# A recurrence in chunks with mixture of depths: PSUM of the state as two tiles, W1 copied by one operation, and the state's chain ahead in the plan

## Chip, cores and metric

The kernel runs on one core of one Trainium2 chip. The metric is device microseconds of one execution of the whole program. Before the change the median of three runs is 329.27 us (327.18 to 331.36).

## What is computed

The first half is a delta rule over 768 tokens for 4 batches of 8 heads with 48 columns each; the second takes the 128 best tokens of each batch through a small expert.

```python
k_n = k / (norm(k) + 1e-6)
for t in range(S):                        # state: 48 x 48 for each batch and head
    y[t] = q[t] @ state
    v_old = state.T @ k_n[t]
    state = state + beta[t] * outer(k_n[t], v[t] - v_old)
x = y of all heads side by side           # (4, 768, 384)
scores = x @ w_gate
out = x
for b in range(4):                        # the 128 tokens of highest score
    xe = x[b, top]
    out[b, top] = xe + sigmoid(scores[b, top]) * (relu(xe @ w1) @ w2)
```

## The kernel before, in words

**Units.** The tokens go in chunks of 64. A unit `i` is one chunk of two batches with all heads (16 pairs of batch and head); there are 24, units 0 to 11 for batches 0 and 1, units 12 to 23 for batches 2 and 3. Within one such half the state goes from unit to unit, so the units of a half run one after the other. Four units make a group `e` (six groups).

**Preparation** (`prep`). q and k are loaded by DMA, turned by TensorE (L399) and copied by ScalarE (L412). TensorE makes the products of k with k (L448, L458), ScalarE copies them to `g` (L464), and from the second group on they go through DRAM (`gd`, L468, L533) to be laid out anew as `a`. The products of q with k (L458 again) are masked on VectorE (L471) to `p`.

**Elimination** (`eliminate`). VectorE inverts the triangular 32x32 blocks of a whole group, row by row (L577, L591, L597), and ends with L602 and in groups 0, 1 and 5 with a transpose (L605). From group 1 on the result comes back by DMA as `tt`, in groups 2 to 4 by way of DRAM (`ad`, L609, L615). `join` makes `z` from it (L679) and copies it to `zt` (L683). Units 0 to 4 and 20 are "direct": they read the result in `g`, by smaller matmuls (L761).

**The chain of the state** (`recur`). For each unit, in this order:
- `mm_r` (L733): the state times k, added in PSUM (`psta`) onto v, which VectorE has scaled and written there (L707); two halves `h4`, each in a bank of its own. The first unit of a half has none.
- `out_r` (L743): ScalarE copies each half to `v`.
- `mm_w` (L755, direct L761): the inverse times that, in two halves, to a PSUM tile `pair`.
- `out_w1` (L779, L781): ScalarE copies the part that the second step needs to `w1`: 96 partitions at once, and two pieces of 32 that change partition.
- `mm_m` (L773): `zt` times `w1` is added; `out_w` (L785) copies the sum to `wbd` in two halves.
- `mm_s` (L795): k times that is added onto the state in `psta`, and `out_s` (L802) copies the state to SBUF in four pieces. The last unit of a half has neither.
- Beside the chain, `mm_q` (L812) and `mm_p` (L824) make the unit's output, L830 copies it, VectorE forms the scores (L842), and L835 writes it out.

**Ranking and expert.** `ranking` compares the scores (L918 to L986) on all engines; `depths` finds the tokens' numbers (L1004), gathers the rows (L1027), turns them (L1033), multiplies by `w1_sb` (L1046) and `w2_sb` (L1062), and scatters the result (L1073). Batches 0 and 1 can start once units 0 to 11 are ranked.

**The order of the work** is made ahead, by a planner in the kernel. Every operation is given to it with its engine, an assumed duration, the operations that it depends on, and a priority (a lower number comes first). `order` plays the program through with these durations, and the instructions are put in each engine's queue in the order of the planned starts; every queue then runs in that order. `pick` takes among the operations that could start first the one of lowest priority; an operation that is marked `hard` keeps later-priority work from starting where that would hold it up by over 0.2 us. The chain is hard. Before, its priority is `u = 10 * i`; q's turn has `10 * i - 20`, the products of q `10 * i - 14`, z `10 * i - 30`, the preparation of group e `40 * e - 100` and its elimination `40 * e - 50`; `mm_q` and `mm_p` have `u + 3`, the ranking of batches 0 and 1 has 148 to 149.2, the expert of batches 0 and 1 260 and more. The planner fills planned gaps of TensorE with matmuls of ones whose result nobody reads (L304).

Of the kernel before, what the change touches and what calls it, by code (L numbers as in the profile page):

```python
# [15 lines left out]
P = 128  # L16
# [141 lines left out]
def kernel(  # L158
# [41 lines left out]
    def sbuf(name, shape, dt=FP32):  # L200
        return const.tile([P] + shape, dt, name=name)
# [41 lines left out]
    rings["one"] = [psum.tile([P, 512], FP32, name=f"one{m}") for m in range(2)]  # L243
    plan.ring("pair", 2)
    plan.ring("one", 2)
    psta = psum.tile([P, 2, 512], FP32, name="psta")

    def got(*key):
        name, m = plan.live[key]
# [38 lines left out]
    nnT = [sbuf(f"nnT{m}", [HC]) for m in range(3)]  # L288
    bh = [sbuf(f"bh{m}", [HC]) for m in range(2)]
    tmp = [sbuf(f"tmp{m}", [HC * HC // 4]) for m in range(2)]  # L290
    w1 = sbuf("w1", [GI, D])
    wbd = [sbuf(f"wbd{m}", [GP, 2, D]) for m in range(2)]
    sts = [sbuf(f"s{m}", [GP, 2, D]) for m in range(2)]
    junk = sbuf("junk", [DM], BF16)
# [21 lines left out]
    four = [(0, 0), (1, 1), (0, 1), (1, 0)]  # L316

    def zero():
        nc.vector.memset(psta[:, :, :GI * D], 0.0)

    def constants():
        nc.vector.memset(warm, 1.0)
# [12 lines left out]
        nc.gpsimd.iota(iota_r, pattern=[[1, CAP]], base=0, channel_multiplier=0,  # L335
                       allow_small_or_imprecise_dtypes=True)

        for b in range(2):
            nc.tensor.matmul(psta[:, b], lhsT=warm[:, :P], rhs=warm, start=True, stop=True)
        zero()  # L340
        nc.vector.memset(pair, 0.0)
        for t in wbd + sts:
# [74 lines left out]
    def prep(i):  # L417
# [89 lines left out]
        else:  # L507
# [3 lines left out]
            n["sg"] = sp(0.6, spill, n["eg"], u, take=[("gd", e)] * (i % BC == 0), lat=4.6)  # L511
            n["sg"].own = 4.2
        v = 10 * i - 14
        n["w"] = pe(0.52, products("qt", kw), n["eq"] + n["ek"] + [N.get(("end", 0))], v,
                    work=1024, take=[kw, ("p", i)], lat=LATE["p"])
        n["ep"] = [dve(0.62, out_p, [n["w"]], v - 200, give=[kw])]

# [174 lines left out]
    def values(i, after):  # L692
        g, c = divmod(i, NCH)
        e, ch = divmod(i, BC)
        n = N[i]

        def vh():
            t = got("v", i)
            by = nnT[e % 3][:, ch * GP:(ch + 1) * GP, None].to_broadcast([P, GP, D])
            if c == 0:  # L700
                nc.vector.tensor_tensor(out=t, in0=t, op=ALU.mult, in1=by)
                return
            to = psta[:, :, GI * D:2 * GI * D].rearrange("p h (b r d) -> p h b r d", b=2, d=D)
            for h in range(2):
                x, y = [z.rearrange("p (h r b) d -> p h b r d", h=2, b=2)[:, h]
                        for z in (t, by)]
                nc.vector.tensor_tensor(out=to[:, h], in0=x, in1=y, op=ALU.mult)  # L707

        n["lv"] = sp(1.38, load(i, "v", (nc.sync,) * 2), prio=10 * i - 35,
                     take=[("v", i)], lat=5.0 if i < 2 else LATE["v"])  # L710
        n["vh"] = dve(0.68 if c > 0 else 0.5, vh, [n["lv"], N["e", e]["nt"], *after],
                      10 * i - 60 if c == 0 else 10 * i - 400)

    def recur(i):
# [3 lines left out]
        hard = dict(hard=True)  # L718
        n, o = N[i], R.get(i - 1, {})
        r = R[i] = {}  # L720
        wb, s_old, s_new = wbd[i % 2], sts[(i + 1) % 2], sts[i % 2]
        kw, ky = ("pair", i, "W"), ("one", i, "Y")

# [4 lines left out]
        def mm_r(h4):  # L728
            def emit():
                for par in range(2):  # L730
                    for bb in range(2):
                        r = bb * 2 + h4
                        nc.tensor.matmul(  # L733
                            psta[half[bb], h4, (GI + 2 * par) * D:(GI + 2 * par + 2) * D],
                            lhsT=got("kt", i)[:, r, half[par]],
                            rhs=s_old[:, r * 2 + par].rearrange("p h d -> p (h d)"),
                            start=False, stop=True, skip_group_check=True)
            return emit


        def out_r(h4):
            def emit():
                nc.scalar.copy(got("v", i)[:, h4 * GI:(h4 + 1) * GI].rearrange("p x d -> p (x d)"),  # L743
                               psta[:, h4, GI * D:2 * GI * D])
            return emit

        def mm_w(h4):
            def emit():
                x, pw = got("v", i), heads(kw)
                for y in range(2 * h4, 2 * h4 + 2):  # L750
                    for bb, par in four:
                        a = 2 * y + par
                        xa = a if c == 0 else y // 2 * 4 + par * 2 + y % 2
                        if not n["direct"]:
                            nc.tensor.matmul(pw[half[par], bb, y],  # L755
                                             lhsT=got("tt", e)[half[bb], ch * GP + a],
                                             rhs=x[half[bb], xa], start=(y == 0), stop=False,
                                             skip_group_check=True)
                            continue
                        for rows in (lo, hi):  # L760
                            nc.tensor.matmul(pw[rows[par], bb, y],  # L761
                                             lhsT=got("g", e)[rows[bb], ch * GP + a, HC:],
                                             rhs=x[rows[bb], xa], start=(y == 0), stop=False,
                                             skip_group_check=True)
            return emit


        def mm_m():
            zt, pw = got("zt", i), heads(kw)
            for y in range(GI):  # L770
                for bb, par in four:
                    rows = at[bb][par]
                    nc.tensor.matmul(pw[hi[par], bb, y], lhsT=zt[rows, y], rhs=w1[rows, y],  # L773
                                     start=False, stop=True, skip_group_check=True)


        def out_w1():
            pw = heads(kw)
            nc.scalar.copy(w1[:3 * HC], pw[:3 * HC, 0])  # L779
            for par in range(2):  # L780
                nc.scalar.copy(w1[hi[par]], pw[lo[par], 1])  # L781

        def out_w(par):
            def emit():
                nc.scalar.copy(wb[half[par], :, par].rearrange("p (b r) d -> p b r d", b=2),  # L785
                               heads(kw)[half[par]])
            return emit

        def mm_s(h4):
            def emit():  # L790
                t = got("k", i)
                for bb in range(2):
                    for rt in range(2):
                        a = bb * 4 + h4 * 2 + rt
                        nc.tensor.matmul(psta[half[rt], h4, bb * 2 * D:(bb + 1) * 2 * D],  # L795
                                         lhsT=t[:, a], rhs=wb[:, a].rearrange("p h d -> p (h d)"),
                                         start=False, stop=True, skip_group_check=True)
            return emit

        def out_s(h4, rt):  # L800
            def emit():
                nc.scalar.copy(  # L802
                    s_new[half[rt], :, rt].rearrange("p (b h x) d -> p b h x d", b=2, h=2)[:, :, h4],
                    psta[half[rt], h4, :GI * D].rearrange("p (b x d) -> p b x d", b=2, d=D))
            return emit

        def mm_q():
# [42 lines left out]
        x = n["vh"]  # L850
        xs = [x]
        if c > 0:
            r["r"] = [pe(0.41, mm_r(h4), [*o["es"][h4], *o["w"], x], u, work=768, **hard)
                      for h4 in range(2)]
            r["xr"] = xs = [act(0.2, out_r(h4), [r["r"][h4]], u, **hard) for h4 in range(2)]
        if i + 1 < NU:
            values(i + 1, [*r.get("xr", []), *o.get("xr", [])])
        clear = N[i + 1]["vh"] if i + 1 < NU else None
# [13 lines left out]
        prev2 = R.get(i - 2, {})  # L872
        r["mw"] = []
        for h4 in range(2):
            r["mw"].append(pe(0.33 if n["direct"] else 0.28, mm_w(h4),
                              [xs[h4 % len(xs)], *n["bk"], *o.get("w", []), *r["mw"]], u,
                              give=[("v", i)] + [("tt", e)] * (e > 0) + [("g", e)] * n["direct"],
                              take=[kw] if h4 == 0 else [], work=384, **hard))
        e1 = act(0.6, out_w1, [*r["mw"], o.get("mm")], u, **hard)
        r["mm"] = pe(0.45, mm_m, [e1, *n["ez"]], u, give=[("zt", i)], work=192, **hard)  # L880
        r["w"] = [act(0.42, out_w(par), [r["mm"], prev2.get("p"), *prev2.get("s", [])], u,
                      give=[kw], **hard) for par in range(2)]
        if not late:
            r["s"] = [pe(0.41, mm_s(h4), [*r["w"], *sum(o.get("es", []), []),
                                          *sum(prev2.get("es", []), []), clear, N.get("zero")],
                         u, work=768, **hard) for h4 in range(2)]
            r["es"] = [[act(0.2, out_s(h4, rt), [r["s"][h4], o.get("q"), *o.get("r", [])], u, **hard)
                        for rt in range(2)] for h4 in range(2)]
        plan.add("PE", 0.0, lambda: None, [*r.get("s", []), n["tk"]], 10 * i, give=[("k", i)])
        qdep = [*r["w"], *r.get("s", [])]  # L890
        pdep = None
        if c > 0:
            r["q"] = pdep = pe(0.81, mm_q, [*sum(o["es"], []), *n["eq"], *r["w"]], u + 3,
                                 take=[ky], work=768)
        r["p"] = pe(0.81, mm_p, [*qdep, *n["ep"], pdep], u + 3, work=1536,
                    take=[] if c > 0 else [ky], give=[("kt", i), ("qt", i), ("p", i)],
                    lat=LATE["x"] if i < NU - 1 else 0.22)
        outs()
# [259 lines left out]
```

## Time and profile before

| | |
|---|---|
| median of 3 runs | 329.27 us (327.18 to 331.36) |
| the profiled execution, its own time | 326.44 us |
| its span, first to last instruction | 324.7 us |
| granted TensorE clock | 0.967 |
| TensorE matmuls busy | 280.9 us (87%) |
| VectorE busy | 220.0 us (68%) |
| ScalarE busy | 159.2 us (49%) |
| GpSimd busy | 26.8 us (8%) |

A line of groups names the source line, the engine and the operation, what is written and what is read (out<-in, buffer numbers left out), partitions x elements, the number of instructions; then their busy time, the mean of one in ns, and the engine's idle time before them with what ended it. A line of the timeline has the start (us from the span's start), the length, the engine, the line, the operation and the count, and in brackets the idle time before it and what ended that. A matmul in fp32 shows as two instructions, so L733 of one unit has 16. PE is TensorE, DVE is VectorE, ACT is ScalarE. In rows of 40 slices each digit is the busy share of a slice of 8.1 us in tenths. The first line that a prediction shows for an operation gives its line number, by which it is found in the code.

### The profile page before, as it was taken

What the parts mean: (1) busy time and instruction counts of PE and PEld (TensorE: products, weight loads), DVE (VectorE), ACT (ScalarE), POOL (GpSimd) and SP (SyncE); (2) the same over time, 40 slices, a digit from 0 to 9 for tenths busy, and PEclk for the clock granted to TensorE, in tenths of its full rate; (3) what the DMA queues carried; (4) which work ended last, traced back from release to release, by engine and by line L of the source; (5) the groups of instructions that cost most, each with busy time, mean ns of one, the idle gap of its engine ahead of it and who ended that gap; (6) DMA issues with size and microseconds to landing.
All of it is one profiled execution on the core that took longest, in us unless ns stands there. A gap on an engine that the chain in (4) does not pass through costs nothing. (4 is left out here: it accounts for less than half of the span.)

```text
span 324.7 us, 16721 instructions
## 1 busy us (share of the span) xinstructions
PE 280.9 (87%) x7306; PEld 205.8 (63%) x7362; DVE 220.0 (68%) x859; ACT 159.2 (49%) x435; POOL 26.8 (8%) x51
## 2 busy tenths in 40 slices
PE   7779997889979898789968898889988889999993
PEld 3545645676657666467647676677767777586571
DVE  6159999998988799969994788997535323432000
ACT  2235415667644765457535566556647647211110
POOL 8111002000100020001000100000020000031011
PEclk9879999999987999889999999999979999999999
DMA  6876978473788758926987993335332021120000
GB/s 99 157 131 153 233 155 142 82 181 58 199 175 143 197 153 177 178 42 151 226 180 139 257 178 64 76 71 96 82 76 52 2 52 25 28 66 36 2 26 24
DMA packets 127545, 37.04 MB, mean 114 GB/s; under 512 B 119536, under 2 KB 123760, under 8 KB 127472
## 3 DMA queue, kind: packets, MB, share of 16 engines
q1 hardware_dynamic: 119904, 33.13, 47.1%
q10 hardware_dynamic: 7056, 1.26, 2.3%
q0 software_dynamic: 512, 1.57, 1.5%
q8 instruction: 58, 0.95, 1.2%
q14 instruction: 15, 0.12, 0.1%
HBM read 22.58 MB, written 12.32 MB: 107 GB/s over the span
## 5 line engine op out<-in xcount | busy, mean ns | idle before, releaser
L304 PE MATMUL one<-warm 128*128 128x512 bf16 x195 | 58.7, 403 | 6.5 <-issue 5.9
L591 DVE TENSOR_TENSOR tmp<-a 128x29 f32<-128x29 f32 (+8 forms) x162 | 55.1, 340 | 0.0
L597 DVE TENSOR_TENSOR a<-a,tmp 128x29 f32<-128x29 f32 (+8 forms) x162 | 53.9, 333 | 0.0
L577 DVE SCALAR_TENSOR_TENSOR a<-a 128x28 f32<-128x28 f32 (+29 forms) x198 | 46.1, 241 | 0.1
L802 ACT COPY s<-psta 64x192 f32<-64x192 f32 x88 | 27.7, 314 | 22.7 <-PE psta L795 21.4
L304 PEld LDWEIGHTS <-warm 128*128 128x128 bf16 x252 | 20.6, 100 | 23.1 <-issue 6.8
L707 DVE TENSOR_TENSOR psta<-v,nnT 128x192 f32<-128x192 f32 x44 | 16.1, 366 | 19.6 <-ACT v L743 18.9
L785 ACT COPY wbd<-pair 64x384 f32<-64x384 f32 x48 | 22.8, 474 | 12.1 <-PE pair L773 9.5
L1046 PE MATMUL pair<-xeT,w_sb 128*64 128x128 f32 x384 | 23.5, 275 | 2.3 <-ACT hT L1053 2.2
L560 POOL TENSOR_SCALAR_AFFINE_SELECT mb<-bh 128x1024 f32<-128x1024 f32 x6 | 10.6, 1759 | 165.8 <-DVE a L602 90.2
L938 DVE TENSOR_SCALAR_CACHE_REDUCE mk<-rep 128x64 bf16<-128x64 f32 (+10 forms) x22 | 13.4, 610 | 15.0 <-ACT rep L931 15.0
L1046 PEld LDWEIGHTS pair<-xeT,w_sb 128*64 128x64 f32 x384 | 20.9, 137 | 3.8 <-ACT hT L1053 3.1
L1062 PE MATMUL one<-w_sb,hT 128*64 128x384 f32 x128 | 22.6, 491 | 0.0
L773 PE MATMUL pair<-w,zt 32*32 32x48 f32 x768 | 13.9, 208 | 9.5 <-ACT w L781 8.7
L795 PE MATMUL psta<-wbd,k 128*64 128x96 f32 x352 | 20.9, 262 | 1.1 <-issue 0.5
L743 ACT COPY v<-psta 128x192 f32<-128x192 f32 x44 | 13.3, 330 | 16.4 <-PE psta L733 16.3
L795 PEld LDWEIGHTS psta<-wbd,k 128*64 128x64 f32 x352 | 16.4, 144 | 7.0 <-ACT wbd L785 4.7
L464 ACT COPY g<-pair 128x512 f32<-128x512 f32 x24 | 13.9, 588 | 13.1 <-PE pair L448 8.2
L773 PEld LDWEIGHTS pair<-w,zt 32*32 32x32 f32 x768 | 10.4, 107 | 15.3 <-ACT w L781 13.9
L824 PE MATMUL one<-wbd,p 128*64 128x96 f32 x384 | 20.0, 247 | 0.0
L1068 DVE SCALAR_TENSOR_TENSOR xe<-one,gate,xe 128x384 f32<-128x384 f32 x4 | 2.5, 617 | 24.8 <-PE one L1062 24.7
L812 PE MATMUL one<-s,qt 128*64 128x96 f32 x352 | 18.6, 248 | 0.0
(116 smaller groups left out, 475.8 us busy)
## 6 DMA issues: line engine op xcount, KB each, us to landing
gd<-g SPq DMA_DIRECT2D x20, 256.0 KB
q<-in_q_dram SPq DMA_DIRECT2D x48, 96.0 KB
v<-in_v_dram SPq DMA_DIRECT2D x48, 96.0 KB
out_dram<-x SPq DMA_DIRECT2D x20, 192.0 KB
k<-in_k_dram SPq DMA_DIRECT2D x36, 96.0 KB
a<-gd SPq DMA_DIRECT2D x20, 128.0 KB
w_sb<-in_moe_w_dram SPq DMA_DIRECT2D x3, 512.0 KB
ad<-a SPq DMA_DIRECT2D x3, 512.0 KB
```

What stands on the lines that cost most here:

```text
L304: nc.tensor.matmul(to if name == "one" else to[:, 0], lhsT=warm[:, :P], rhs=warm, start=True, stop=True)
L577: nc.vector.scalar_tensor_tensor(out=to, in0=of, scalar=by, in1=to, op0=ALU.mult, op1=ALU.add)
L591: nc.vector.tensor_tensor(out=view(), op=ALU.mult, in0=x[0].to_broadcast(shape), in1=x[1].to_broadcast(shape))
L597: nc.vector.tensor_tensor(out=to, in0=to, in1=view(), op=ALU.add)
L773: nc.tensor.matmul(pw[hi[par], bb, y], lhsT=zt[rows, y], rhs=w1[rows, y], start=False, stop=True, skip_group_check=True)
L785: nc.scalar.copy(wb[half[par], :, par].rearrange("p (b r) d -> p b r d", b=2), heads(kw)[half[par]])
L795: nc.tensor.matmul(psta[half[rt], h4, bb * 2 * D:(bb + 1) * 2 * D], lhsT=t[:, a], rhs=wb[:, a].rearrange("p h d -> p (h d)"), start=False, ...
L802: nc.scalar.copy(s_new[half[rt], :, rt].rearrange("p (b h x) d -> p b h x d", b=2, h=2)[:, :, h4], psta[half[rt], h4, :GI * D].rearrange(" ...
L812: nc.tensor.matmul(got(*ky)[half[bb], :2 * GI * D] .rearrange("p (h r x d) -> p h x r d", h=2, r=2, x=2)[:, h4, par], lhsT=got("qt", i)[:, ...
L824: nc.tensor.matmul(py[half[bb], x * 2 * D:(x + 1) * 2 * D], lhsT=t[:, a], rhs=wb[:, a].rearrange("p h d -> p (h d)"), start=(c == 0 and x ...
L1046: nc.tensor.matmul(ps[half[x]], lhsT=w1_sb[:, t, c0:c0 + C], rhs=got("xeT", b)[:, t], start=(t == 0), stop=(t == KD - 1))
L1062: nc.tensor.matmul(got("one", b, "o")[c0:c1, :DM], lhsT=got("hT", b)[:, f, c0:c1], rhs=w2_sb[:, f], start=(f == 0), stop=(f == KF - 1))
```

## The change

There are three edits. The state's PSUM `psta`, one tile of two banks, becomes two tiles of one bank each, and every use of `psta[:, h4]` becomes `psta[h4]`. The second batch's part of W (bank 1) now begins at column 0 and the first's (bank 0) at column 192; in the units that are not direct, `mm_w` makes the part of the second batch that `w1` needs once more, on the partitions where it is wanted, in columns 192 to 383 of bank 1. So `out_w1` is one copy of 128 partitions and 2 x 192 columns there, and `w1` has a place for each of the two batches. Direct units keep three copies. Last, the chain's operations get the priority `uc = u - 35`, and most of its assumed durations are altered. `mm_q` and `mm_p` keep `u + 3`.

```diff
-    psta = psum.tile([P, 2, 512], FP32, name="psta")
+    psta = [psum.tile([P, 512], FP32, name=f"psta{h}") for h in range(2)]
...
-    w1 = sbuf("w1", [GI, D])
+    w1 = sbuf("w1", [2, GI, D])
+    bank0, bank1 = GI * D, 512
...
-        for b in range(2):
-            nc.tensor.matmul(psta[:, b], lhsT=warm[:, :P], rhs=warm, start=True, stop=True)
+        for t in [*psta, *[t[:, 1] for t in rings["pair"]]]:
+            nc.tensor.matmul(t, lhsT=warm[:, :P], rhs=warm, start=True, stop=True)
...
-        n["w"] = pe(0.52, products("qt", kw), n["eq"] + n["ek"] + [N.get(("end", 0))], v,
+        n["w"] = pe(0.58, products("qt", kw), n["eq"] + n["ek"] + [N.get(("end", 0))], v,
...
+        uc = u - 35
...
+        def w_of(bb):
+            x = got(*kw).rearrange("p b x -> p (b x)")[:, (bank1, bank0)[bb == 0]:]
+            return x[:, :GI * D].rearrange("p (r d) -> p r d", d=D)
...
+                    for par in range(0 if direct else 2):
+                        a = 2 * y + par
+                        xa = a if c == 0 else y // 2 * 4 + par * 2 + y % 2
+                        nc.tensor.matmul(again[hi[par], y], lhsT=t[half[1], ch * GP + a, :HC],
+                                         rhs=x[half[1], xa], start=False, stop=True,
+                                         skip_group_check=True)
...
         def out_w1():
-            pw = heads(kw)
-            nc.scalar.copy(w1[:3 * HC], pw[:3 * HC, 0])
+            if not n["direct"]:
+                nc.scalar.copy(w1.rearrange("p b r d -> p b (r d)"),
+                               got(*kw)[:, :, GI * D:2 * GI * D])
+                return
+            nc.scalar.copy(w1[:3 * HC, 0], w_of(0)[:3 * HC])
             for par in range(2):
-                nc.scalar.copy(w1[hi[par]], pw[lo[par], 1])
+                nc.scalar.copy(w1[hi[par], 1], w_of(1)[lo[par]])
...
-            r["r"] = [pe(0.41, mm_r(h4), [*o["es"][h4], *o["w"], x], u, work=768, **hard)
+            r["r"] = [pe(0.38, mm_r(h4), [*o["es"][h4], *o["w"], x], uc, work=768, **hard)
                       for h4 in range(2)]
-            r["xr"] = xs = [act(0.2, out_r(h4), [r["r"][h4]], u, **hard) for h4 in range(2)]
+            r["xr"] = xs = [act(0.22, out_r(h4), [r["r"][h4]], uc, **hard) for h4 in range(2)]
...
-            r["mw"].append(pe(0.33 if n["direct"] else 0.28, mm_w(h4),
-                              [xs[h4 % len(xs)], *n["bk"], *o.get("w", []), *r["mw"]], u,
+            r["mw"].append(pe(0.33 if n["direct"] else 0.37, mm_w(h4),
+                              [xs[h4 % len(xs)], *n["bk"], *o.get("w", []), *r["mw"]], uc,
...
-        e1 = act(0.6, out_w1, [*r["mw"], o.get("mm")], u, **hard)
-        r["mm"] = pe(0.45, mm_m, [e1, *n["ez"]], u, give=[("zt", i)], work=192, **hard)
-        r["w"] = [act(0.42, out_w(par), [r["mm"], prev2.get("p"), *prev2.get("s", [])], u,
+        e1 = act(1.0 if n["direct"] else 0.38, out_w1, [*r["mw"], o.get("mm")], uc, **hard)
+        r["mm"] = pe(0.47, mm_m, [e1, *n["ez"]], uc, give=[("zt", i)], work=192, **hard)
+        r["w"] = [act(0.47, out_w(par), [r["mm"], prev2.get("p"), *prev2.get("s", [])], uc,
...
-            r["s"] = [pe(0.41, mm_s(h4), [*r["w"], *sum(o.get("es", []), []),
+            r["s"] = [pe(0.36, mm_s(h4), [*r["w"], *sum(o.get("es", []), []),
...
-            r["es"] = [[act(0.2, out_s(h4, rt), [r["s"][h4], o.get("q"), *o.get("r", [])], u, **hard)
+            r["es"] = [[act(0.32, out_s(h4, rt), [r["s"][h4], o.get("q"), *o.get("r", [])], uc, **hard)
...
-            r["q"] = pdep = pe(0.81, mm_q, [*sum(o["es"], []), *n["eq"], *r["w"]], u + 3,
+            r["q"] = pdep = pe(0.68, mm_q, [*sum(o["es"], []), *n["eq"], *r["w"]], u + 3,
...
-        r["p"] = pe(0.81, mm_p, [*qdep, *n["ep"], pdep], u + 3, work=1536,
+        r["p"] = pe(0.76, mm_p, [*qdep, *n["ep"], pdep], u + 3, work=1536,
```

## The prediction, as put on record

> **What bounds the kernel now.** I read the page, then the timeline of TensorE (PE) and ScalarE (ACT) around one unit, then the start times of each unit's stages, then the waits for DMA, then the tail. The page:
>
> ```profile
> span 324.7 us, 16721 instructions
> ...
> PE   7779997889979898789968898889988889999993
> ...
> DVE  6159999998988799969994788997535323432000
> ...
> L304 PE MATMUL one<-warm 128*128 128x512 bf16 x195 | 58.7, 403 | 6.5 <-issue 5.9
> ```
>
> TensorE looks full, but 58.7 us of it are L304, matmuls that only fill planned gaps. VectorE is dense until slice 27 (222 us), where the sixth elimination ends. So in between I must see whether the units wait for VectorE or for each other. One unit (16) in the timeline; start, length, engine, line:
>
> ```profile
> 202.67 0.88 PE L795 MATMUL psta<-wbd,k 128*64 128x96 f32 x16
> 203.38 0.83 PE L812 MATMUL one<-s,qt 128*64 128x96 f32 x16
> 203.59 1.29 ACT L802 COPY s<-psta 64x192 f32<-64x192 f32 x4 [0.51 <-PE psta L795]
> 204.04 0.83 PE L824 MATMUL one<-wbd,p 128*64 128x96 f32 x16
> 204.80 0.46 PE L399 MATMUL pair<-ident,q 64*128 64x64 f32 x8
> 205.19 0.88 PE L733 MATMUL psta<-s,kt 128*64 128x96 f32 x16
> 206.12 0.32 ACT L743 COPY v<-psta 128x192 f32<-128x192 f32 x1 [1.23 <-PE psta L733]
> 206.71 0.60 ACT L412 COPY qt<-pair 128x512 f32<-128x512 f32 x1
> 207.18 0.35 ACT L743 COPY v<-psta 128x192 f32<-128x192 f32 x1
> 207.62 0.45 PE L755 MATMUL pair<-v,tt 64*64 64x48 f32 x16
> 208.21 0.32 ACT L779 COPY w<-pair 96x192 f32<-96x192 f32 x1 [0.68 <-ACT v L743]
> 208.56 0.64 ACT L781 COPY w<-pair 32x192 f32<-32x192 f32 x2
> 209.25 0.54 PE L773 MATMUL pair<-w,zt 32*32 32x48 f32 x32 [0.70 <-ACT w L781]
> 209.73 1.25 PE L304 MATMUL one<-warm 128*128 128x512 bf16 x5
> 210.91 0.45 PE L679 MATMUL pair<-tt,g 32*32 32x32 f32 x32
> 211.29 0.88 PE L795 MATMUL psta<-wbd,k 128*64 128x96 f32 x16
> ```
>
> The cycle takes 8.62 us (202.67 to 211.29). The first ACT copy of `psta` at 206.12 follows the end of all 16 matmuls of L733 (206.07), though it needs the first eight only, and the two copies L743 have L412 between them. L824 and L399 stand ahead of L733, L679 ahead of L795. Stage by stage (first L755/L761 of a unit): unit 12 at 172.8, 16 at 206.5, 20 at 245.4, 23 at 273.3, and its L830 ends at 279.5. Unit 20 needs only the sixth elimination, done by 221.9 (L605), and starts 23.5 us later: from unit 12 on the units wait for each other. Before that they wait for VectorE and DMAs (units 4, 5, 8). Unit 11 is different:
>
> ```profile
> 164.40 0.45 PE L679 MATMUL pair<-tt,g 32*32 32x32 f32 x30 [0.64 <-DMA tt<-ad]
> ...
> 166.02 0.68 PE L755 MATMUL pair<-v,tt 64*64 64x48 f32 x32
> ```
>
> Its copies L743 ended at 160.7, but L755 stood behind L679 of units 12 and 13, which waited for a DMA. Last, the tail: three batches of the expert run from 284.2 to 319.8 with little gap, 11.85 us each, and the span ends 5.0 us later. So TensorE's order sets the end.
>
> **The skill.** TensorEngine Tiling (Array Packing), Key Properties: changing the tiling mode drains TensorE. The trace agrees: 64x64 matmuls of L755 start in groups of four 58 ns apart, but from 64x128 (L399) to 64x64 (L458) 151 ns pass, from L755 to L399 149 ns. PSUM — Partial Sum Buffer, PSUM bank collisions raise a hardware error: engines collide on one bank and quadrant, different banks run clean. So the wait of L743 for the second half of L733 comes from the tile's being one, not from the chip. ScalarE: Activation LUTs, What ACT_TABLE_LOAD costs: 186 ns + 0.833 ns per element, 506 ns for 384; the trace has 487 ns for 128x384 (L830), which I use.
>
> **The change, part by part**, for one cycle.
> 1. *Two tiles.* L743 may follow the first eight matmuls of L733, L802 those of L795. First saving 0.41 us (half of L733's 0.83 to the end). The second is counted in 2. If the split does nothing, both go.
> 2. *Chain first on TensorE.* L733 starts 2.52 us after L795 now. The first two copies L802 can end at 0.44 + 0.05 + 2 x 0.32 = 1.13; L812 still fits and ends at 0.88 + 0.66 = 1.54; saved 0.98. L679 leaves its place: 0.38. L824 (0.66), L399 (0.39) and L679 (0.38), 1.43 us, go to where ACT copies: 1.25 us of L304 at 209.73 and 0.59 at 207.10 cover them. In units whose gaps hold ranking or expert work instead, up to 0.5 comes back; I add 0.5 everywhere. A wait that may grow: when L755 heads the queue and waits for the DMA of tt (units 5, 8, 12, 16), the turns and products of k behind it wait, and with them the next elimination on VectorE. L679 already stands there (1.67 us at 95.54), so I count nothing, at most 2 us a time.
> 3. *Chain first on ScalarE.* L412 leaves the pair of L743; the second L755 now starts 1.13 us after the first, and could at 0.35; but see 4. Taken 0.25 (0.06 to 0.48).
> 4. *W1.* Three copies from 208.21 to 209.20, 0.97, become one of 384 elements, 0.48: saves 0.49. For it each L755 half gets four more matmuls of 64x32. The trace has none between 64x64. Low: no drain, +0.09 a half, what the plan's own costs raise. High: three more changes of mode a half at 110 ns beyond the usual spacing and two groups of 58: 0.45. I take 0.42 a half, as 64x128 to 64x64 has the same 64 rows and drains. One half hides under the second L743, so +0.42, up to 0.9. Alone this part gains between -0.4 and +0.4. Six units (0 to 4, 20) keep their three copies.
> 5. *The rest* costs nothing: two more warm-up matmuls and a split memset lie in the start-up, where VectorE and DMAs are waited for; uncovered, below 1 us. No DMA is added. L389's load of v waits for the chain to release a buffer, and L609 is queued behind it on SP (issued at 153.91, eliminated by 146.8), so a faster chain helps; counted at nothing. POOL's table L560 and its gathers are not moved.
>
> Sum: -0.41 - 0.98 - 0.38 - 0.25 - 0.49 + 0.42 + 0.5 = -1.6; the cycle falls from 8.62 to 7.0.
>
> **Along the run.** Units 0 to 8 keep their bounds: no gain. Unit 12 cannot start before its zt (165.3): 166, gain 6.8. Unit 16: 166 + 28 = 194, but its L679 ran at 195.8 on the DMA of tt: 196. Unit 20: 224, at its elimination. Unit 21's zt came at 232.1, so 232; then 239, 246 and the last L830 6 us later: C = 252. Ranking and table loads made units 17 to 20 longer than 8.6 (9.7 from 206.5 to 245.4, 4.4 in all, and part of it will stay with more ahead of it in line); I add 6: C = 258, 21 us less. What is late next is the expert: four batches of 11.85 and 1.2 us of ranking after C, and 5 to the span's end: C + 53.6, less what runs before C. Before, 8.4 us did (333.1 - 324.7). xeT of batch 0 is there at 248.8; with the chain ahead I take 2. Span 258 + 53.6 - 2 = 309.6. The profiled execution took 326.44 for 324.7, 1.7 more: 311.3; the median of the runs, 329.27, stands 2.8 above it: 314.
>
> **Rivals.**
> - *B, full gaps.* The cycle has about 6.9 us of TensorE work: the chain L733 0.81, L755 0.66 + 0.84, L773 0.54, L795 0.81, and the rest L812, L824, L399, L679, L458 2.7 and ranking 0.5. Its short gaps do not hold it; chain operations wait for z, the masked products and each other as before. Then half the gain is left: C = 268, span 319.6, time 325. For it: in the stretch 205.19 to 213.82 TensorE is busy for 7.35 of 8.63 us. Against: up to 1.8 us of that is L304.
> - *C, slower: the expert is pushed behind a chain that got no shorter.* The place is 254.7 to 279.5, where L1046 and L1062 now run between chain steps. If mode changes cost the high end (+0.4 net) and the reordering yields nothing, C = 281 and all four batches follow: 281 + 53.6 + 4.5 = 339. It decides from C = 278 (slower by 2%). Against: L824 and L399 ahead of L733 are plainly there to be moved.
> - *D, the split does nothing.* If L743 goes on waiting for all of L733, the 11 cycles from unit 12 lose 0.41 each, 4.5 us: 318.5. The waits at 206.12 and 203.59 are what to look at.
>
> **How the numbers follow.** About 2% is what a measurement of this kernel can tell from no change: 322.7 and 335.9. The likeliest case, with D inside it, has 0.70 and its own range is 306 to 322; B 0.18, 323 to 332; C 0.12. The low end, 304, is C = 252 (308) with the sixth elimination 4 us earlier (VectorE stood 3.4 us for the DMA a<-gd at 179.2); the high end, 328, leaves out C and the upper part of B.
>
> **What would show it.** Right: L733 directly behind L812; L743 starting near the middle of L733; no L412 between the two; one copy of 128x384 of about 0.48 us to w1; cycles near 7 us from unit 12 to 22; L755 of unit 11 before the L679 of unit 12; the first L755/L761 of unit 20 near 224 to 230; the last L830 near 258; after it an unbroken row of L1046 and L1062. Wrong: L755 with its additions taking under 0.4 us a half (part 4 too dear) or over 0.8 (too cheap); unit 20 still 20 us behind its elimination; eliminations ending later because turns and products of k came late; TensorE gaps after the last L830.

## The result, and the profile after

The changed kernel takes 334.76 us (median of 20 runs, 330.49 to 339.61), the kernel before 328.81 in the same comparison (20 runs, 325.53 to 333.36). The ratio is 1.016, its 95% interval 1.013 to 1.019: slower by 1.6%, where I had forecast 314 and a range up to 328. That is less than the 2% that the prediction wanted for telling two kernels apart, but the interval leaves no doubt of the sign. Ratios and intervals are those on record for the faster runs of each kernel, so they need not be the quotients of the medians beside them. The profiled execution of the changed kernel took 337.52 us, at a granted clock of 0.946.

The page of the changed kernel, in the lines shown of before, and last the granted clock (in tenths, 9 for 90% or more), changed and then before:

```profile
span 335.8 us, 17190 instructions
...
PE   7799889999789988499997999999989999999994
...
DVE  6179999989948799518896458988925555511000
...
L305 PE MATMUL one<-warm 128*128 128x512 bf16 x149 | 44.9, 406 | 5.3 <-issue 5.2
...
PEclk9799999999979999569999599999979999999998
```

```profile
PEclk9879999999987999889999999999979999999999
```

TensorE is fuller (busy 298.6 us, before 280.9), although 13.8 us of useless matmuls (L305, before L304) have gone. VectorE now has holes in slices 11, 16, 17, 22 and 23 (counted from 0) and stays dense until slice 28: the eliminations end later. TensorE runs at half its clock from 135.7 to 149.4 us and from 183.5 to 193.7; between 20 us and the end of its work these stretches add up to 30.7 us, before to 13.6.

The two traced executions differ by 11.1 us in their spans. The last L830, where the chain has ended (the prediction's C), comes at 280.8 in place of 279.5. What lies behind it has grown from 45.2 to 55.0. So the chain, which was to end 21 us earlier, has gained nothing, and the expert stands behind it.

Unit 16 again, from the state's matmuls of unit 15 (L817, before L795) to the copy of W1 (L796, before L779 and L781), in the timeline of the changed kernel:

```profile
209.06 0.88 PE L817 MATMUL psta<-wbd,k 128*64 128x96 f32 x16 [0.32 <-ACT wbd L806]
209.66 1.30 ACT L824 COPY s<-psta 64x192 f32<-64x192 f32 x4 [0.65 <-PE psta L817]
209.87 0.46 PE L401 MATMUL pair<-ident,q 64*128 64x64 f32 x8
210.35 1.21 PE L736 MATMUL psta<-s,kt 128*64 128x96 f32 x16
210.98 0.32 ACT L746 COPY v<-psta 128x192 f32<-128x192 f32 x1
211.20 0.59 ACT L414 COPY qt<-pair 128x512 f32<-128x512 f32 x1
211.49 0.33 PE L767 MATMUL pair<-v,tt 64*64 64x48 f32 x8
211.68 0.34 ACT L746 COPY v<-psta 128x192 f32<-128x192 f32 x1
211.75 0.28 PE L780 MATMUL pair<-v,tt 64*32 64x48 f32 x4
211.96 0.33 PE L767 MATMUL pair<-v,tt 64*64 64x48 f32 x8
212.22 0.28 PE L780 MATMUL pair<-v,tt 64*32 64x48 f32 x4
212.75 0.33 PE L767 MATMUL pair<-v,tt 64*64 64x48 f32 x8 [0.25 <-ACT spr L940]
213.01 0.28 PE L780 MATMUL pair<-v,tt 64*32 64x48 f32 x4
213.22 0.33 PE L767 MATMUL pair<-v,tt 64*64 64x48 f32 x8
213.48 0.28 PE L780 MATMUL pair<-v,tt 64*32 64x48 f32 x4
213.84 0.48 ACT L796 COPY w<-pair 128x384 f32<-128x384 f32 x1 [1.35 <-issue]
```

The split does what it says: the first copies of L824 and L746 start while L817 and L736 still run. L736 starts 1.29 us after L817, before 2.52. But the two halves of `mm_w` now take from 211.49 to 213.68, where the next matmuls start, and within each half the tile shape changes three times, between 64x64 (L767) and 64x32 (L780). From first to last start a half takes 0.80 us (median of its 36) against 0.23 before; both halves take 1.73 where nothing comes between them, against 0.46. Over the run, in the groups of the changed kernel, then of the kernel before:

```profile
L767 PE MATMUL pair<-v,tt 64*64 64x48 f32 x576 | 25.7, 244 | 9.5 <-DMA tt<-ad 5.8 <-DVE a L599 1.7 <-DMA tt<-g 0.8
L780 PE MATMUL pair<-v,tt 64*32 64x48 f32 x288 | 20.6, 222 | 0.0
L796 ACT COPY w<-pair 128x384 f32<-128x384 f32 x18 | 8.6, 480 | 43.3 <-PE pair L780 39.8 <-issue 3.4
```

```profile
L755 PE MATMUL pair<-v,tt 64*64 64x48 f32 x576 | 14.0, 227 | 2.0 <-ACT v L743 1.7 <-ACT qt L412 0.2
L779 ACT COPY w<-pair 96x192 f32<-96x192 f32 x24 | 7.6, 315 | 16.1 <-PE pair L755 9.0 <-PE pair L761 3.1 <-DVE a L602 2.3
```

The 576 matmuls that were busy for 14.0 us are so for 25.7, with 20.6 us of L780 beside them. And ScalarE now stands 39.8 us for L780 ahead of its 18 copies, where it stood 9.0 for L755. Two waits stand out besides. SP's queue is held for the landing of a load of beta that ScalarE issues; VectorE stands for `a` and for `v`. SP's longest such waits (all of the run); VectorE's from 140 to 200 us; and the latter in the kernel before:

```profile
SPq L391 <- DMA bt<-in_beta_dram: 12.5, 2, 12.2
```

```profile
DVE psta L709 <- ACT v L746: 13.5, 7, 5.6
DVE nrm L541 <- DMA a<-gd: 7.8, 1, 7.8
```

```profile
DVE psta L707 <- ACT v L743: 3.7, 4, 1.6
DVE nrm L539 <- DMA a<-gd: 3.4, 1, 3.4
```

A line has the total in us, the times and the longest. The hold of 12.2 us lies at 106 to 119 us. Behind it on SP, L611 (before L609) goes out at 127.4, before 119.5, though that elimination had ended at about the same time (112.7 and 113.7). So TensorE meets unit 8's L767 before its `tt`:

```profile
131.91 1.25 PE L305 MATMUL one<-warm 128*128 128x512 bf16 x5
137.43 0.41 PE L767 MATMUL pair<-v,tt 64*64 64x48 f32 x2 [4.26 <-DMA tt<-ad]
```

`a` of the next group comes at 146.7 in place of 138.4, and the rows of the running elimination stand behind it on VectorE. The last L604 (before L602) of the six eliminations ends at 46, 79, 113, 155, 188 and 238 us; before at 47, 81, 114, 147, 174 and 219.

### The profile page after: what moved, and what is told of

Same layout as the page of the kernel before. It is cut to its first block, busy times and chain, and to the rows that moved or that the text cites. A ratio compares the mean times of both kernels' runs of the same rounds, so it can differ in the third digit from the quotient of the medians.

```text
span 335.8 us, 17190 instructions
## 1 busy us (share of the span) xinstructions
PE 298.6 (89%) x7553; PEld 221.1 (66%) x7593; DVE 219.9 (65%) x861; ACT 151.4 (45%) x399; POOL 27.0 (8%) x51
## 5 line engine op out<-in xcount | busy, mean ns | idle before, releaser
L593 DVE TENSOR_TENSOR tmp<-a 128x29 f32<-128x29 f32 (+8 forms) x162 | 53.7, 332 | 0.0
L305 PE MATMUL one<-warm 128*128 128x512 bf16 x149 | 44.9, 406 | 5.3 <-issue 5.2
L767 PE MATMUL pair<-v,tt 64*64 64x48 f32 x576 | 25.7, 244 | 9.5 <-DMA tt<-ad 5.8
L824 ACT COPY s<-psta 64x192 f32<-64x192 f32 x88 | 27.6, 313 | 13.7 <-PE psta L817 12.5
L796 ACT COPY w<-pair 128x384 f32<-128x384 f32 x18 | 8.6, 480 | 43.3 <-PE pair L780 39.8
L767 PEld LDWEIGHTS pair<-v,tt 64*64 64x64 f32 x576 | 16.4, 139 | 16.0 <-issue 8.9
L305 PEld LDWEIGHTS <-warm 128*128 128x128 bf16 x193 | 16.0, 101 | 16.5 <-issue 3.5
L817 PE MATMUL psta<-wbd,k 128*64 128x96 f32 x352 | 20.8, 264 | 1.2 <-ACT wbd L806 1.0
L846 PE MATMUL one<-wbd,p 128*64 128x96 f32 x384 | 21.5, 256 | 0.0
L817 PEld LDWEIGHTS psta<-wbd,k 128*64 128x64 f32 x352 | 16.5, 145 | 6.8 <-ACT wbd L806 4.4
L780 PE MATMUL pair<-v,tt 64*32 64x48 f32 x288 | 20.6, 222 | 0.0
L414 ACT COPY qt<-pair 128x512 f32<-128x512 f32 x24 | 14.0, 590 | 13.0 <-PE pair L401 9.8
L834 PE MATMUL one<-s,qt 128*64 128x96 f32 x352 | 19.1, 251 | 0.2 <-ACT x L852 0.2
```

The costliest lines, as they stand in the source:

```text
L305: nc.tensor.matmul(to if name == "one" else to[:, 0], lhsT=warm[:, :P], rhs=warm, start=True, stop=True)
L593: nc.vector.tensor_tensor(out=view(), op=ALU.mult, in0=x[0].to_broadcast(shape), in1=x[1].to_broadcast(shape))
L767: nc.tensor.matmul(w_of(bb)[half[par], y], lhsT=t[half[bb], ch * GP + a], rhs=x[half[bb], xa], start=(y == 0), stop=False, skip_group_chec ...
L780: nc.tensor.matmul(again[hi[par], y], lhsT=t[half[1], ch * GP + a, :HC], rhs=x[half[1], xa], start=False, stop=True, skip_group_check=True)
L817: nc.tensor.matmul(psta[h4][half[rt], bb * 2 * D:(bb + 1) * 2 * D], lhsT=t[:, a], rhs=wb[:, a].rearrange("p h d -> p (h d)"), start=False, ...
L824: nc.scalar.copy(s_new[half[rt], :, rt].rearrange("p (b h x) d -> p b h x d", b=2, h=2)[:, :, h4], psta[h4][half[rt], :GI * D].rearrange(" ...
```

## The experiments

Times are medians; ratios are to the kernel before on the same chip, with intervals. From each trace I also read: C, the end of the last L830 (by whatever line it has there), as in the prediction; the rest of the span after C; the end of the sixth elimination's L602, behind which its transpose L605 ends about 2 us later; and the mean cycle, unit 13 to 19, between first matmuls of `mm_r`. These four are of one execution, whose own time stands in the column "traced" and can lie off the median. The kernel before took 328.44 in the comparison of e1 to e4, 326.11 in that of e5 to e8 and 329.45 in that of e9 to e12.

| kernel | us | ratio (interval) | traced | C | after C | sixth elimination | cycle |
|---|---|---|---|---|---|---|---|
| before | 328.81 | 1 | 326.44 | 279.5 | 45.2 | 219.4 | 8.56 |
| changed | 334.76 | 1.016 (1.013 to 1.019) | 337.52 | 280.8 | 55.0 | 238.3 | 8.56 |
| e1_split | 320.05 | 0.972 (0.967 to 0.977) | 322.97 | 275.8 | 45.2 | 217.0 | 8.18 |
| e2_w1 | 333.90 | 1.019 (1.014 to 1.024) | 333.52 | 282.0 | 49.8 | 220.0 | 9.63 |
| e3_prio | 351.48 | 1.066 (1.062 to 1.071) | 352.03 | 292.9 | 56.7 | 253.2 | 8.20 |
| e4_no_w1 | 319.19 | 0.970 (0.966 to 0.974) | 321.15 | 265.0 | 54.4 | 222.7 | 8.02 |
| e5_dur | 332.93 | 1.021 (1.011 to 1.031) | 325.93 | 268.9 | 55.3 | 224.4 | 8.54 |
| e6_64 | 324.28 | 0.996 (0.992 to 1.000) | 329.99 | 273.3 | 55.0 | 230.1 | 7.88 |
| e7_group | 327.92 | 0.998 (0.994 to 1.002) | 326.69 | 270.0 | 54.9 | 229.7 | 8.03 |
| e8_beta | 324.68 | 0.981 (0.972 to 0.990) | 330.31 | 271.5 | 57.1 | 231.2 | 8.97 |
| e9_beta_no_w1 | 315.40 | 0.959 (0.951 to 0.968) | 311.95 | 253.4 | 56.8 | 216.0 | 7.53 |
| e10_64_beta | 316.16 | none | 314.39 | 255.6 | 57.1 | 216.3 | 7.59 |
| e11_split_dur | 318.63 | 0.970 (0.964 to 0.977) | 317.92 | 266.1 | 48.6 | 214.4 | 8.06 |
| e12_prio_dur | 336.58 | 1.021 (1.012 to 1.030) | 338.55 | 282.5 | 54.3 | 237.3 | 8.94 |

The first four take the change apart. Two theories stood against each other: W, that the W1 edit is too dear, and Q, that queues which wait for late DMAs lose the time.

**The split alone.** In the kernel before, `psta` is two tiles, as in the first lines of the diff.

> The kernel before with the state's PSUM as two tiles, nothing else; the plan's order is unchanged. If the split acts, L743's copy starts after the first eight matmuls of L733 and the state's copies after the first eight of L795: up to 0.8 us a cycle where the order lets it, so 323 to 328 us. If the split does nothing: 327 to 331. It cannot be what made the changed kernel slower by either theory.

320.05 us, a gain of 8.4 and more than I expected. The cycle falls by 0.38 us, and C by 3.7 in the profiled execution. In the timeline of this kernel L744 (before L743) starts 0.60 after the first matmul of its L734; before, L743 started 0.93 after.

```profile
203.73 0.88 PE L734 MATMUL psta<-s,kt 128*64 128x96 f32 x16
...
204.33 0.32 ACT L744 COPY v<-psta 128x192 f32<-128x192 f32 x1 [1.21 <-PE psta L734]
```

**The W1 edit alone**, with its two durations (0.37; 0.38 and 1.0).

> The kernel before with only the W1 edit and its two assumed durations. Theory W (the added 64x32 matmuls with their mode changes cost TensorE about 0.5 us a half and more than the saved copies give back): slower, 332 to 337 us. Theory Q (the loss came from queues that wait for late DMAs, set off by the new order): near the kernel before, 327 to 332.

333.90 us, 5.5 more than the kernel before: as theory W has it. The sixth elimination ends as before (220.0). The cycle from unit 13 to 19 is 1.07 us longer, but over units 13 to 23 only 0.15 (9.44 against 9.29): C comes 2.5 us later, and what follows C is 4.6 us longer, as the expert's first matmul comes at 268.7 in place of 254.7.

**The priority alone**, old durations.

```diff
+        uc = u - 35
...
-            r["r"] = [pe(0.41, mm_r(h4), [*o["es"][h4], *o["w"], x], u, work=768, **hard)
+            r["r"] = [pe(0.41, mm_r(h4), [*o["es"][h4], *o["w"], x], uc, work=768, **hard)
```

and so `uc` for `u` in every operation of the chain.

> The kernel before with only the chain's priority lowered by 35, old durations. Theory Q: the order alone makes eliminations late (the sixth ends at 232 us or later instead of 221.9) and pushes the expert behind the chain: 331 to 338 us. Theory W: the order alone gains, as I had predicted for it: 315 to 323.

351.48 us, worse than theory Q's upper end. The sixth elimination ends at 253.2. VectorE stands for `v` 19 times, SP is held twice by loads of beta (12.7 and 10.9 us).

**The changed kernel without the W1 edit.**

> The changed kernel with W1 copied by three operations as before (its matmuls, copies and their two assumed durations of before), two tiles and the new order kept. Theory W: the loss goes and the gain of the order shows: 315 to 324 us. Theory Q: still slow, 329 to 336, with SP's queue held again for the landing of a load of beta and the sixth elimination ending after 230.

319.19 us, as theory W has it: beside the other edits the W1 edit takes all that they gain, and 4.6% of the time (0.970 to 1.016). That is 15.6 us, where alone it took 5.5: most of its price comes from what it meets. The sixth elimination ends at 222.7, though SP is held here too (10.4 us at 70, 7.0 at 116), so a hold alone does not make it late. The starts of `mm_r` show where the time goes:

| first matmul of `mm_r` of unit | 8 | 9 | 19 | 23 |
|---|---|---|---|---|
| before | 125.4 | 141.5 | 230.4 | 272.0 |
| changed | 115.5 | 149.6 | 232.6 | 270.7 |
| e4_no_w1 | 119.9 | 139.3 | 223.0 | 255.8 |
| e8_beta (below) | 115.6 | 140.5 | 225.2 | 260.0 |

At unit 8 the changed kernel is 4.3 us ahead of the one without the W1 edit, at unit 9 it is 10.3 us behind, and at unit 23 14.9. So two thirds of the loss fall at one place: unit 8 waits for its `tt`, and half clock follows. Why the hold ahead of it is longer with the W1 edit than without (12.2 us at 106, against 7.0 at 116) was not followed up.

The next four ask what is dear in the W1 edit, and what SP's hold costs.

**The plan told of the true length.**

```diff
-            r["mw"].append(pe(0.33 if n["direct"] else 0.37, mm_w(h4),
+            r["mw"].append(pe(0.33 if n["direct"] else 0.92, mm_w(h4),
-        e1 = act(1.0 if n["direct"] else 0.38, out_w1, [*r["mw"], o.get("mm")], uc, **hard)
+        e1 = act(1.0 if n["direct"] else 0.48, out_w1, [*r["mw"], o.get("mm")], uc, **hard)
```

> The changed kernel with other assumed durations for the W1 edit alone: a half of mm_w 0.92 us in place of 0.37 (which is what its L767 and L780 take in the trace), the copy 0.48 in place of 0.38. The work is the same, the plan knows its length. Theory P (the loss is mostly that the plan puts VectorE's and the queues' operations too early, and they wait): 320 to 328 us. Theory M (the added time on TensorE itself, 18 units of about 1 us less the 0.5 saved, is what is lost): 329 to 336.

332.93 us, in the range of theory M, but the six executions lie between 325.93 and 339.00, and the trace is of the fastest: its row of the table is no reading of the median. No gain is shown; whether a small one hides in the spread stays open.

**The added matmuls with their neighbours' shape.**

```diff
-                        nc.tensor.matmul(again[hi[par], y], lhsT=t[half[1], ch * GP + a, :HC],
+                        nc.tensor.matmul(again[half[par], y], lhsT=t[half[1], ch * GP + a],
```

> The changed kernel with the added matmuls made 64x64 like their neighbours (32 more columns, whose results nobody reads): as many instructions, the same planned order, no change of tile shape inside mm_w. Theory M (changes of shape are the cost): a half takes about 0.45 us in place of 0.93, the loss goes, 312 to 321 us. Theory N (the number of added matmuls is the cost): 330 to 336.

In this kernel the wanted rows come out in the lower half of each 64, so `w1` holds other data for the second batch; the amount of work is as said. 324.28 us, ratio 0.996. A half takes 0.46 us from first to last start in place of 0.80. Theory M holds in kind, and the time stays 3 us above its range; SP's hold of 10.9 us at 108 is still there, and unit 9 starts at 148.4.

**One change of shape in place of three.** The loop over `par` moves behind the loop over `y`, so that a half's four added matmuls stand at its end.

> The changed kernel with the four added 64x32 matmuls of a half behind one another at its end: the same instructions in another order, one change of shape inside a half in place of three. Theory M: about half of the loss of the W1 edit goes, 322 to 330 us. Theory N: unchanged, 331 to 336.

327.92 us, in the range of theory M. In the timeline of this kernel, two halves (of the second, the view shows the first six of L780):

```profile
211.48 0.45 PE L767 MATMUL pair<-v,tt 64*64 64x48 f32 x16
211.86 0.36 PE L780 MATMUL pair<-v,tt 64*32 64x48 f32 x8
...
212.47 0.45 PE L767 MATMUL pair<-v,tt 64*64 64x48 f32 x16
212.85 0.32 PE L780 MATMUL pair<-v,tt 64*32 64x48 f32 x6
```

A half takes 0.54 us, two changes fewer save 0.26, so 0.13 us each. In the trace of the changed kernel 148 ns pass from the last start of L767 to the first of L780, and 132 ns on the way back, where 38 ns pass between two groups of L755 in the kernel before. The same matmuls in another order are worth 1.8% (1.016 to 0.998). SP's hold (12.9 us at 106), the wait for `tt` (3.7 us at 137) and a sixth elimination at 229.7 are here as well.

**Beta's loads by GpSimd.**

```diff
-            betas(e, act, nc.scalar, [N["e", e - 1]["rt"]], 40 * e - 82)
+            betas(e, pool, nc.gpsimd, [N["e", e - 1]["rt"]], 40 * e - 82)
```

> The changed kernel with beta's loads of groups 1 to 5 issued by GpSimd instead of ScalarE, so that SP's queue need not wait for their landing. Theory Q (SP's hold of 12.2 us at 106 us makes the DMAs, and with them the eliminations, late): 322 to 329 us, the second elimination's tt lands near 131, not 139. If the hold only takes the place of another wait: 331 to 336.

324.68 us, ratio 0.981: the hold is gone, TensorE does not stand for `tt` at 137, and unit 9's first matmul comes at 140.5 in place of 149.6. Theory Q is right too. How much the holds cost beside the W1 edit is less sure: 3.5% by the ratios (1.016 to 0.981), 2.2% by the medians (334.76 to 328.81 is 1.018; 324.68 to 326.11 is 0.996, above the interval of the ratio, 0.972 to 0.990). Its trace is of the slowest of five executions.

The last four combine.

**Without the W1 edit and with beta by GpSimd.**

> Two tiles and the new order with W1 copied as before, and beta's loads issued by GpSimd. In the trace of the same kernel with beta on ScalarE, SP's queue is held for 10.4 us at 70 us and 7.0 us at 116 us. Theory Q (the holds make eliminations late): 310 to 316 us. If other waits take their place: 317 to 322.

315.40 us, ratio 0.959: the fastest here, and in the range of theory Q. The interval 0.951 to 0.968 touches that without the move of beta (0.966 to 0.974), so a gain of about 1% is likely rather than sure. In the trace, which is of the fastest of four executions, C is 253.4 and the cycle 7.53, where the prediction had 258 and 7.0 for the change itself.

**Both repairs of the changed kernel.** The stationary operand of an added matmul takes the 32 columns ahead of its block as well, so the wanted rows come out in the upper half.

> The changed kernel with two repairs: the added matmuls are 64x64 with the wanted rows in their place (one that has no column block ahead of it stays 64x32), and beta's loads are issued by GpSimd. Theories M and Q together: the two halves of mm_w take 0.92 us from first to last start in place of 1.73, no hold of SP over 8 us before 150 us: 312 to 319 us. If copying W1 at once is worth its 0.5 us a unit once it costs no change of shape, below the kernel with two tiles, new order and beta on GpSimd; if not, above it.

316.16 us, in the range of both theories together: a half takes 0.46 us, and no load of beta holds SP. There is no interval for this kernel, so this and the one before are told apart by nothing: 0.2% lie between their medians. No gain or loss by copying W1 at once is shown then.

**The split and the durations, the priority as before.**

> Two tiles and the new assumed durations (without those of the W1 edit), the chain's priority as before. If the priority has the gain beyond the split: as the split alone, 319 to 324 us. If the durations have it: 315 to 320. If both are worth nothing beyond the split: equal to the split alone within 1%.

318.63 us, 0.970, the same as with the new priority (e4_no_w1, 0.970) and as the split alone (0.972). Neither the priority nor the durations are worth anything on top of the split here; whether the priority is, once beta is loaded by GpSimd, no run shows. In the traces C differs by 1.1 us only; after C the span is 54.4 with the priority and 48.6 without, and the expert of batch 0 starts at 260.3 in place of 252.2.

**The priority and the durations without the split.**

> The kernel before with the chain's lowered priority and the new assumed durations, without the split and the W1 edit. If the loss of the priority with the old durations (ratio 1.066) came from the plan's running ahead of the chip: 322 to 331 us, few waits of VectorE for L743. If the priority itself is bad for this kernel: 338 to 352.

336.58 us, between the two theories, nearer to the second. The durations take 15 us off the time of e3_prio (351.48), and the priority without the split still loses 2.1%. VectorE's waits, in this kernel and then in the same with the split (e4_no_w1); the kernel before has 18.9 us of them:

```profile
DVE psta L707 <- ACT v L744: 32.4, 16, 6.3
```

```profile
DVE psta L708 <- ACT v L745: 19.8, 24, 3.7
```

L707 is the product for the next unit, which is queued on VectorE among the rows of an elimination. When the chain is later than the plan has it, VectorE stands there and the elimination with it. The split brings the copy that it waits for forward on the chip, not in the plan. That this is why the priority loses without the split fits the two lines; no run tests it by itself.

## Why the prediction was wrong, by its own steps

- **Part 4, W1, failed in size, and this turned the sign.** I priced a half at +0.42 us, hid the other under the second copy, and let the edit gain or lose 0.4 us a cycle. A half is dearer by 0.57 (0.23 to 0.80), and nothing hides the first: both halves went from 0.46 to 1.73, so +1.27, beyond the 0.9 that I allowed, against the 0.49 that the copies gave back (0.97 to 0.48). I had named the cause, the change of shape, and my 110 ns beyond the usual is near what the trace has (148 and 132 against 38). The error was mostly the hidden half. Without the edit the kernel gains 3.0% (e4_no_w1), with it it loses 1.6%. The net of 0.78 us in each of 18 units makes 14 us, and 15.6 were lost; that these agree is chance. Up to unit 8 nothing was lost, at unit 8 about 14.6 us at one stroke, and alone the edit cost 5.5 us.
- **"Units 0 to 8 keep their bounds" failed.** It took the DMAs and VectorE as fixed. Unit 8 came 9.9 us earlier than before and unit 9 8.1 us later. In the sum I had counted at nothing that SP's L389 holds up L609, and that TensorE's queue stands at L755 for `tt`. The second happened at unit 8 (4.26 and 1.53 us, I had said at most 2 a time). The first came to 12.2 us, through a landing of beta, which I had not seen although the trace of before has holds of 5.5 and 6.6 us by it. e8_beta prices this at 2.2 to 3.5%. The sixth elimination came 19 us late. Unit 20 starts its `mm_w` at 242.4, 1.6 us after that elimination's transpose (240.8), where it came 23.5 us after it before; a wait for it does not show.
- **Parts 2 and 3, the order, brought little.** A saving of 1.6 us a cycle (0.98, 0.38 and 0.25), less 0.5, was expected beyond the 0.41 of the split. The split alone has cycles of 8.18, e11_split_dur 8.06 and e4_no_w1 8.02. L736 does stand nearer to L817, but L401 and not L834 stands between, and L414 still stands between the two copies L746. In e4_no_w1 C comes at 265.0, but the stretch behind it grows. In the changed kernel the expert could not have begun much before C: the turned rows of its first batch are there at 270.1, before at 248.8. In e9_beta_no_w1, with beta loaded by GpSimd, the cycle is 7.53, so part of the saving was there to be had.
- **Part 1, the split, was right in kind; its size stays open.** I counted 0.41 us a cycle, 4.5 us over eleven; the cycle fell by 0.38, and the median by 8.4. The two traced executions differ by only 3.5 us (326.44 and 322.97), which eleven such cycles cover. The other 5 us lie between these executions and the medians, and no trace shows them.
- **The tail was nearly right.** C + 53.6 less 2, so 51.6 after C, was forecast; measured are 55.0, and 54 to 57 for the kernels with the new priority. With C = 258 the time would have stayed in the range; C was 280.8. Rival C, to which I gave a chance of 0.12, had C = 281 and a time of 339, where 334.76 was measured. Its account, a chain that got no shorter and an expert behind it, is what came, though its price for W1 (+0.4 a cycle) was half of what the matmuls and copies show (+0.8), and the loss at unit 8 was not in it.

## What to carry to other kernels

Adding small matmuls of another tile shape inside a stream costs time at every change (here about 0.13 us), so group them or give them their neighbours' shape, even if half of the result is not read. The price of an edit depends on what stands beside it: the same one cost 5.5 us alone and 15.6 us together with the others, so look at where in the run the units lose their time before multiplying a cost by the number of units. Before a chain is put first in a plan, look at what it is queued with on the other engines: here each unit's product on VectorE and the loads on SP tie eliminations, DMAs and chain together. With the old durations the priority alone cost 6.6%, with the new ones 2.1%, and on top of the split it gained nothing. One tile of two banks can hold up a copy for matmuls that write the other bank; of the three edits measured alone (split, W1, priority) only the split gained (2.8%).

## What the runs showed of the hardware

- A change between 64x64 and 64x32 matmuls costs about 0.13 us, though both use 64 rows; as many 64x64 matmuls, with twice the output rows and no change, are cheaper (0.46 against 0.54 us a half).
- TensorE's granted clock falls to 0.5 for stretches of 3.4 us and more. Some follow a time in which TensorE stood: in e7_group 6.8 us at 137.5, behind waits of 3.7 and 1.1 us; in the kernel before 6.8 us at 95.4, at a wait of 1.67 us; in the changed kernel 13.7 us at 135.7, at a wait of 4.26. Others do not: in e2_w1 6.8 us at 218.7, with no idle time of TensorE over 0.8 us near it, and in e9_beta_no_w1 a wait of 1.6 us at 162 was followed by none. So these traces give no rule for it, and no run here holds the clock still.
- The time of one kernel can go with the granted clock: the five executions of e8_beta took 330.31, 327.41, 324.68, 321.92 and 320.41 us at 0.959, 0.970, 0.979, 0.989 and 0.992. In the changed kernel the two go together more loosely (330.49 at 0.962, 333.04 at 0.976).
- A load of 4 KB queued on ScalarE held SP's queue for up to 12.9 us, as SP waited for its landing before it issued a load of its own. Why these two are tied I did not test; issuing beta from GpSimd took the tie away.
